# Seven products instead of eight for five pairs of slices of a feed-forward layer, with helping operations placed by due times

## The chip, the cores and the metric

The program runs on one core of one Trainium2 chip (the kernel is built for a single core). The metric is device time in microseconds (us) of one execution; several executions are given by their median.

The engines are named as in the profile: PE is TensorE (matrix products), DVE is VectorE, ACT is ScalarE, POOL is GpSimd, SP is SyncE, which issues the DMA transfers.

## The reference

Attention over clusters gives 1536 tokens of 512 numbers; two feed-forward layers follow. Both are shown whole, as the change and the stretches of time around it lie in them.

```python
def _moe_ref(x, w_in, w_out):                      # layer 1: 512 -> 2048 -> 512
    h = x @ w_in
    beta = 1.0
    neg = h <= -beta
    pos = h >= beta
    g = np.where(pos, h, np.where(neg, 0.0, (h + beta) ** 2 / (4.0 * beta)))
    return (g @ w_out).astype(np.float32)

def _moe2_ref(x, w_gate, w_val, w_out, rms_g):     # layer 2: 512 -> 1536 -> 512
    rms = np.sqrt(np.mean(x * x, axis=-1, keepdims=True) + 1e-06)
    xn = x / rms * rms_g
    g = xn @ w_gate
    silu = g * (1.0 / (1.0 + np.exp(-g)))
    val = xn @ w_val
    return (silu * val @ w_out).astype(np.float32)
```

## The kernel before, in words

**Numbers in two parts.** Every fp32 operand of a product is held as a high and a low part of type fp32r. One product of a 128-row stationary tile with 512 columns is three matmuls: high by high, high by low, low by high.

**Tiles.** The tokens lie in three blocks of 512 (`NB`, `BLK`), numbered 0, 1 and 2. Layer 1 has 16 slices of 128 hidden units, layer 2 has 12. `h_unit(layer, m, b)` makes slice m of the hidden units for block b: four 128-row pieces of X times three, 12 matmuls into one PSUM bank (`proj`, L624). Then come the gate on ACT (L639, L640) and DVE (L641), the rounding to a high part on ACT (L668) and the low part on DVE (L665). `y_unit` multiplies the results of a group of slices with slices of the second matrix, for 128 tokens at a time (L786 to L788); the sum over groups is kept in SBUF in Y (ACT copies the first group, L800, DVE adds the later ones, L802). The groups of layer 1 are `GROUPS1`.

**Weights.** SP loads every slice of a weight matrix twice, 512 KB each, once as it is (`raw`, L521) and once shifted by two bytes (`mid`, L523). There are two buffers for each, and a slice's conversion must end before the next load into its buffers can start. The conversion takes one ACT and six DVE operations (L565, then L566, L568, L570, L576, L578, L580) and puts the slice into one of 24 SBUF places.

**Layer 2 already multiplies in seven products.** Blocks 0 and 1 against the two halves of the contraction and two weight slices would take eight half products; sums and differences of X and of the weights make seven do (`term_unit`, with the table `TERMS`; PE line L651). The sums of the weights are made on POOL by `w_sums` (L534, 256 columns wide), and the parts on ACT and DVE (L557, L559). Partial results that are used twice are copied from PSUM to SBUF by ACT (L713, names u, e, v, w) and added in by DVE (L716) and by POOL (L719). Layer 1 uses none of this: POOL stands still through most of it.

**Order.** All engines run their own queues in the order in which the program writes the instructions. A list of units (`units`) sets the order on PE; the helping operations are written between them by a pace: so much of DVE's time (`pace["dve"]`, `cost`, `fill`) for so much of PE's, with stages of a unit's follow-up work in `later`, released by `drain`.

## Time and profile before

| | us |
|---|---|
| median of 3 executions (lowest, highest) | 777.17 (776.75, 777.27) |
| the profiled execution | 775.95 |
| its span in the trace | 774.2 |
| busy: PE, DVE, ACT, POOL | 768.3, 609.9, 391.9, 288.9 |
| layer 1 begins on PE at | 230.5 |

The granted TensorE clock is 0.999 over the span. A line of the timeline reads: start in us after the start of the span, duration in us, engine, line of the program, operation, output<-inputs, shape, and in brackets how long the engine had been idle and what ended that. `aa`, `bb` and `place` are SBUF places of converted slices or of gated results; `raw`, `mid` and `bits` belong to a conversion in progress; `h`, `y`, `A`, `B`, `E` are PSUM banks.

### The profile page before, as it was taken

How to read it: one execution, taken by the hardware profiler on the slowest of the kernel's cores; microseconds unless marked ns; L12 is line 12 of the kernel's file. 1: busy time of each engine (PE TensorE's matmuls, PEld its weight loads, DVE VectorE, ACT ScalarE, POOL GpSimd, SP SyncE). 2: the span in 40 equal slices, each digit the busy share in tenths (PEclk: the TensorE clock that was granted, in tenths of full speed). 3: DMA queues.
4: the chain of work that ended last, by engine and by line, in shares of the span. 5: the costliest groups of instructions: out<-in, count | busy, mean ns of one | idle time of the engine just before them, and what ended most of it. 6: DMA issues, size and time to landing. Idle time of an engine off the chain costs nothing.

```text
span 774.2 us, 10868 instructions
## 1 busy us (share of the span) xinstructions
PE 768.3 (99%) x3714; PEld 592.0 (76%) x3714; DVE 609.9 (79%) x1106; ACT 391.9 (51%) x758; POOL 288.9 (37%) x313
## 2 busy tenths in 40 slices
PE   8999999999999999999999999999999999999998
PEld 4666666776558888888888888878888888888887
DVE  6776887776578999877668768899999799988743
ACT  7676767665567655444334447544545315423430
POOL 5878999998000000000001206441454334423400
PEclk9999999999999999999999999999999999999999
DMA  7657665573144676444334310125563343434013
GB/s 202 173 138 182 156 150 131 150 172 113 55 142 143 218 237 218 170 137 163 109 109 136 99 37 0 32 95 181 187 213 109 104 160 128 154 109 163 1 41 123
DMA packets 32679, 103.41 MB, mean 134 GB/s; under 512 B 5016, under 2 KB 5356, under 8 KB 32624
## 3 DMA queue, kind: packets, MB, share of 16 engines
q1 hardware_dynamic: 32612, 102.72, 43.8%
q8 instruction: 29, 0.48, 0.3%
q14 instruction: 26, 0.21, 0.1%
q10 hardware_dynamic: 12, 0.00, 0.0%
HBM read 81.02 MB, written 3.15 MB: 109 GB/s over the span
## 4 chain that ended last, share of the span: by engine, by line
PE 92%; DVE 2%; ACT 2%; DMA 1%; POOL 1%; issue 1%; ACTq 0%; DVEq 0%; POOLq 0%
PE h L624 25%; PE y L788 9%; PE y L787 9%; PE y L786 9%; PE pv L406 8%; PE B L651 8%; PE mp L336 5%; PE sc L385 4%; PE sc L386 4%; PE E L651 4%; PE A L651 2%; PE sum L425 1%; DMA kraw<-kT 1%; PE simt L171 1%; PE sum L414 1%
## 5 line engine op out<-in xcount | busy, mean ns | idle before, releaser
L338 DVE TENSOR_REDUCE M<-mp 128x1 f32<-128x384 f32 x186 | 94.6, 552 | 44.6 <-PE mp L336 44.4
L534 POOL TENSOR_TENSOR bits<-place 128x256 f32<-128x256 f32 x18 | 17.6, 1000 | 265.5 <-DVE place L580 265.5
L398 POOL TENSOR_TENSOR acc<-acc,P 128x384 f32<-128x384 f32 x112 | 109.2, 1004 | 4.1 <-ACT P L388 3.5
L388 ACT ACTIVATE P<-sc 128x384 f32<-128x384 f32 x192 | 82.3, 490 | 42.1 <-PE sc L386 34.1
L624 PE MATMUL h<-xh,aa 128*128 128x512 f32 x280 | 89.3, 390 | 0.1
L802 DVE TENSOR_TENSOR Y<-y,Y 128x512 f32<-128x512 f32 (+1 forms) x85 | 57.8, 681 | 39.6 <-PE y L788 39.3
L639 ACT ACTIVATE a<-h,half_b 128x512 f32<-128x512 f32 x48 | 33.0, 687 | 81.4 <-PE h L624 80.4
L406 PE MATMUL pv<-P,v 128*64 128x384 f32 x384 | 70.6, 492 | 0.0
L385 PE MATMUL sc<-aa,bb 112*128 112x384 f32 x192 | 66.1, 344 | 0.0
L386 PE MATMUL sc<-aa,bb 97*128 97x384 f32 x192 | 65.0, 338 | 0.0
L624 PE MATMUL h<-xh,bb 128*128 128x512 f32 x200 | 64.2, 389 | 0.0
L624 PEld LDWEIGHTS h<-xh,aa 128*128 128x128 f32 x280 | 52.5, 188 | 12.9 <-DVE a L641 0.8
L565 ACT ACTIVATE raw<-raw 128x512 f32<-128x512 f32 x62 | 42.2, 680 | 38.1 <-DMA raw<-w_out 12.4
L641 DVE SCALAR_TENSOR_TENSOR a<-h,a 128x512 f32<-128x512 f32 x48 | 33.1, 690 | 29.7 <-ACT a L640 29.7
L624 PE MATMUL h<-xl,aa 128*128 128x512 f32 x140 | 54.5, 389 | 0.0
L568 DVE SCALAR_TENSOR_TENSOR bits<-raw,bits 128x512 uint32<-128x512 uint32 x68 | 51.7, 760 | 1.6
L336 PE MATMUL mp<-bb,aa 112*128 112x384 f32 x186 | 52.5, 360 | 0.3
L406 PEld LDWEIGHTS pv<-P,v 128*64 128x64 f32 x384 | 25.4, 136 | 31.4 <-issue 30.3
L336 PEld LDWEIGHTS mp<-bb,aa 112*128 112x128 f32 x186 | 32.2, 189 | 15.3 <-issue 5.5
L624 PEld LDWEIGHTS h<-xh,bb 128*128 128x128 f32 x200 | 37.5, 188 | 7.8
L719 POOL TENSOR_TENSOR w<-w,e 128x512 f32<-128x512 f32 x12 | 16.8, 1396 | 60.9 <-ACT w L713 60.9
L624 PE MATMUL h<-xl,bb 128*128 128x512 f32 x100 | 38.9, 389 | 0.0
(307 smaller groups left out, 1987.3 us busy)
## 6 DMA issues: line engine op xcount, KB each, us to landing
...
```

The source lines that it names most:

```text
L336: nc.tensor.matmul(mp, A[0:112, h, 0, 128 * qt:128 * qt + 128], Bk[0:112, h, 0, HALF * n:HALF * n + HALF], start=True, stop=True)
L338: nc.vector.tensor_reduce(st["M2", p][:, j, n:n + 1], mp, axis=AX.X, op=ALU.max)
L385: nc.tensor.matmul(sc, Bk[0:112, h, 0, ks], A[0:112, h, 0, qs], start=True, stop=False)
L386: nc.tensor.matmul(sc, Bk[0:97, h, 1, ks], A[0:97, h, 1, qs], start=False, stop=True)
L388: nc.scalar.activation(P, sc, AF.Exp, scale=0.125)
L398: nc.gpsimd.tensor_tensor(acc, acc, P, op=ALU.add)
L406: nc.tensor.matmul(pv[64 * h:64 * h + 64, 0:HALF], st["v", p][:, h, kt], st["P", p, i, h], start=(kt == 0), stop=(kt == NT - 1))
L624: nc.tensor.matmul(h, w[:, wi, fs], x[:, kc, cs], start=(n == 0), stop=(n == 11))
L651: nc.tensor.matmul(h, w[:, wi, fs], x[xi][:, kc], start=start and n == 0, stop=(n == 5), skip_group_check=not start)
L786: nc.tensor.matmul(y[:, c], g[:, 0, fs], w[:, 0, c], start=(m == m0), stop=False)
L787: nc.tensor.matmul(y[:, c], g[:, 0, fs], w[:, 1, c], start=False, stop=False)
L788: nc.tensor.matmul(y[:, c], g[:, 1, fs], w[:, 0, c], start=False, stop=(m == ms[-1]))
```

## The change

Layer 1 gets the seven products for blocks 0 and 1, in five pairs of slices: (3, 4), (5, 6), (7, 8), (9, 10) and (11, 12). Block 2 and the other slices keep whole products. Per pair, two sums of POOL (512 columns, L725) and four (256 columns, L739 to L742) make the weights' sums `s1_m_0` and `s1_m_1`; ACT and DVE split each into parts (L702, L703). X needs three more sums and a changed block 1: `x_parts` makes them once (L979 and L982 on POOL, L982 and L990 on DVE, L989 on ACT), overwriting the first half of block 1's X; `x_back` restores it before the last slices of block 1 (L954 to L962). ACT copies the partial results of a pair from PSUM (L917), DVE (L923) and POOL (L928) add them in.

The conversion of a slice is done in another way: two ACT operations (L708, L709) and five DVE operations (L710 to L714).

The helping operations are no longer paced. Each is a task with a due time; while the program is built, a plan with a clock for each engine and a price for each kind of operation (`KINDS`) chooses what is written next into which queue. The units on PE are sorted by a table of numbers, `ORDER`.

```diff
-GROUPS1 = [3, 3, 4, 3, 3]
+GROUPS1 = [3, 4, 3, 3, 3]
...
-LOCK = 0.3
+AFTER = 12
+SQP = ()
+LOCKED = 1.15
+KEEP, YD, GD, ROUND, XD = 1.5, 6.0, 6.0, 6.0, 2.0
+ORDER = (
+    0, 1, 2, 3, 4, 5, 6, 7, 8, 9, 10, 11, 12, 13, 14, 15, 16, 17, 18, 19, 20, 21, 22, 23, 24, 25, 26, 27, 28,
+    29, 30, 31, 33, 34, 32, 35, 36, 37, 38, 39, 40, 41, 42, 43, 44, 45, 46, 47, 48, 49, 50, 53, 51, 52, 54,
...
+NEAR, DUE, CONV = 0.1, 8.0, 4.0
+LOAD, LAND = 4.2, 0.8
...
+             "tt": ("dve", 0.6, 0.74), "t256": ("dve", 0.335, 0.47), "tiny": ("dve", 0.08, 0.2),
+             "p512": ("pool", 1.28, 1.4), "p256": ("pool", 0.74, 0.85)}
...
+        clock[e] = at + busy * (LOCKED if e == "dve" and clock["pool"] > at else 1.0)
...
+        hi, mid, t, sq = cv.pop(n)
+        tf, bits = t.bitcast(F32), sq.bitcast(U32)
+        v = nc.vector
+        task(landed[n], op("copy", lambda: nc.scalar.activation(sq, hi.bitcast(F32), AF.Copy, scale=2.0 ** -112), (("y", n),)),
+             op("copy", lambda: nc.scalar.activation(hi.bitcast(F32), hi.bitcast(F32), AF.Sign), (("sg", n),)), due=due_of(key))
+        task(landed[n], op("t256", lambda: v.tensor_scalar(mid, mid, 0x01FFFFFF, None, op0=ALU.bitwise_and)),
+             op("t256", lambda: v.tensor_scalar(t, bits, 3, 0x7FFFF000, op0=ALU.logical_shift_left, op1=ALU.bitwise_and), (), (("y", n),)),
+             op("tt", lambda: v.tensor_tensor(w[:, 0], tf, hi.bitcast(F32), op=ALU.mult), (("w0", key),), (("sg", n),)),
+             op("t256", lambda: v.tensor_scalar(t, w[:, 0].bitcast(U32), 0xFF800000, None, op0=ALU.bitwise_and)),
+             op("tt", lambda: v.scalar_tensor_tensor(w[:, 1], mid, 2.0 ** -36, tf, op0=ALU.mult, op1=ALU.mult), (("w1", key),)),
+             due=due_of(key), end=load_next)
+        if layer == 2 and i < 2:
+            w_sums(2, i, m, key, w, tf)
+        if layer == 1 and i == 0 and GROUPS1[0] <= m < M1 - GROUPS1[-1]:
+            w_sums(1, 1 - m % 2, m - 1 + m % 2, key, w, tf)
+
...
+        first = op("p512", lambda: g(f, w[:, 0].bitcast(F32), w[:, 1].bitcast(F32), op=ALU.add), (("f", layer, i, m),), (("w0", key), ("w1", key)))
...
+        task(0.0, first, op("p256", lambda: g(tile_of(k1)[:, left], f2[:, left], f2[:, right], op=ALU.add), (), (("f", layer, 0, m),)),
+             op("p256", lambda: g(fp[k1][:, right], fp[k1][:, left], f1[:, left], op=ALU.subtract), (k1,)),
+             op("p256", lambda: g(tile_of(k2)[:, left], f1[:, left], f2[:, left], op=ALU.subtract)),
+             op("p256", lambda: g(fp[k2][:, right], f1[:, right], fp[k1][:, right], op=ALU.subtract), (k2,)), due=due_of(key))
...
+    def term_unit(layer, k, m):
         c, _, half, start = TERMS[k]
+        w = need(key_of(layer, k, m))
+        row, b = ENDS.get(k, (0, 0))
+        n = m + row if layer == 1 else m
+        if k in ENDS and (layer == 1 or row):
+            G[layer, n, b] = take()
...
+        if k in (6, 7, 4, 3):
+            wait_for(("keep", {6: "u", 7: "v", 4: "w", 3: "e"}[k], layer, m))
...
+        if k in (1, 5, 6):
+            task(now(1.36), kept("uev"[(1, 5, 6).index(k)]), due=now(1.36) + KEEP)
+            return
+        both = op("p512", lambda: nc.gpsimd.tensor_tensor(C["w", m], C["w", m], C["e", m], op=ALU.add), (("used", "e", layer, m),), (("keep", "e", layer, m),))
+        first = {2: (plus("u"),) if k == 2 else (), 3: (plus("v"),) if k == 3 else (), 7: (kept("w"), both) if k == 7 else (), 4: ()}[k]
+        end_ = ("used", "w", layer, m) if k == 7 else bank
+        if layer == 1:
+            last = gated(n, b, (lambda: C["w", m]) if k == 7 else (lambda: src), end_)
...
+    def x_parts():
...
+        def add(i, j, kc, b):
+            cs = slice(BLK * b, BLK * b + BLK)
+            nc.gpsimd.tensor_tensor(get(i, j), XH[:, kc + j, cs].bitcast(F32), XL[:, kc + j, cs].bitcast(F32), op=ALU.add)
+
+        def minus(e, i, j, x, y):
+            e.tensor_tensor(get(i, j), get(x, j), get(y, j), op=ALU.subtract)
+
+        for j in range(2):
+            dst = [(XH[:, j, b1], XL[:, j, b1]), (h3[:, j], l3[:, j]), (h2[:, j], l2[:, j]), (h4[:, j], l4[:, j])]
+
+            def hilo(i, part, j=j, dst=dst):
+                h, l = dst[i]
+                return (op("copy", lambda: nc.scalar.copy(h, get(i, j)), (("xh", i, j),), (("p", i, j),)),
+                        op("tt", lambda: nc.vector.tensor_tensor(l, get(i, j), h.bitcast(F32), op=ALU.subtract), (("xt", part, j),)))
+
+            g, v = nc.gpsimd, nc.vector
+            task(now(0.0), op("p512", lambda j=j: add(1, j, 0, 1)), op("p512", lambda j=j: add(0, j, 0, 0)),
+                 op("p512", lambda j=j: minus(g, 0, j, 1, 0), (("p", 0, j),)), due=now(0.0) + XD + 0.1 * j)
+            task(now(0.0), *hilo(0, 1), due=now(0.0) + XD + 0.1 * j)
+            task(now(0.0), op("p512", lambda j=j: add(2, j, 2, 1), (), (("p", 0, j),)),
+                 op("tt", lambda j=j: minus(v, 1, j, 2, 1), (("p", 1, j),)),
+                 op("tt", lambda j=j: minus(v, 2, j, 2, 0), (("p", 2, j),)), due=now(0.0) + XD + 0.1 * j)
+            task(now(0.0), *hilo(1, 3), due=now(0.0) + XD + 0.2)
+            task(now(0.0), *hilo(2, 2), due=now(0.0) + XD + 0.2)
+            task(now(0.0), op("p512", lambda j=j: add(3, j, 2, 0), (), (("p", 0, j),)),
+                 op("p512", lambda j=j: minus(g, 3, j, 3, 2), (("p", 3, j),), (("p", 2, j),)), *hilo(3, 4), due=now(0.0) + XD + 0.2)
...
+        def pair_of(m):
+            g, s, r = (1, 0, m), (1, 0, -m - 1), (1, 1, -m - 1)
+            return [term(1, 1, m), h(1, m, 2), term(1, 2, m), end(g), term(1, 5, m), term(1, 6, m), end(s), h(1, m + 1, 2), term(1, 3, m), term(1, 7, m), end(r)]
+
+        def last_pair(m):
+            return [term(1, 4, m), end((1, 0, m + 1))]
...
+        hz = [h(1, m, b) for b in range(NB) for m in range(GROUPS1[0])]
+        yield from (*hz[:7], xs(0), *hz[7:], *(done(1, m) for m in range(GROUPS1[0])))
+        zs = ys(1, 0)
+        yield from zs
+        a, b, c, d, e = (pair_of(m) for m in range(3, 13, 2))
+        yield from (*a, b[0], *last_pair(3), *b[1:])
+        zs = ys(1, 1)
+        yield (tables, 0.0, 0.0, [], 0)
+        yield from (zs[0], *last_pair(5), *zs[1:], *c, d[0], *last_pair(7), *d[1:])
+        zs = ys(1, 2)
+        yield from (zs[0], *last_pair(9), *zs[1:], *e)
         n = len(GROUPS1) - 1
         new = range(sum(GROUPS1[:n]), M1)
-        yield from (*ys(1, n - 1, 0), *hs(1, new, 0), *ys(1, n - 1, 1), *hs(1, new, 1), *ys(1, n, 0))
+        hz, ws = hs(1, new, 0), ys(1, n - 1, 0)
+        yield from (hz[0], *last_pair(11), back(0), back(1), hz[1], hz[2], *ws, *ys(1, n - 1, 1), *hs(1, new, 1), *ys(1, n, 0))
...
+    work[:] = [work[i] for i in ORDER]
```

Three places show what that does to the queues. The first is POOL after the last product of attention (`acc6_7_1`, L421; L398 before). Before:

```order
L398 TENSOR_TENSOR acc6_7_1_2571<-acc6_7_1_2571,P6_11_1_2658 128x384
L534 TENSOR_TENSOR bits32_4430<-place3_3131 128x256 x2
L534 TENSOR_TENSOR bits33_4459<-bb0_106 128x256 x2
L534 TENSOR_TENSOR s0_0_4565<-bits33_4459 128x256
L534 TENSOR_TENSOR s0_0_4565<-s0_0_4565,bits32_4430 128x256
L534 TENSOR_TENSOR s0_1_4566<-bits32_4430,bits33_4459 128x256
L534 TENSOR_TENSOR s0_1_4566<-bits32_4430,s0_0_4565 128x256
```

and with the change:

```order
L979 TENSOR_TENSOR p1_0_3160<-xh_103,xl_104 128x512
L979 TENSOR_TENSOR p1_1_3162<-xh_103,xl_104 128x512
L979 TENSOR_TENSOR p0_0_3164<-xh_103,xl_104 128x512
L979 TENSOR_TENSOR p0_1_3182<-xh_103,xl_104 128x512
L982 TENSOR_TENSOR p0_0_3164<-p1_0_3160,p0_0_3164 128x512
L982 TENSOR_TENSOR p0_1_3182<-p1_1_3162,p0_1_3182 128x512
L979 TENSOR_TENSOR p2_0_3218<-xh_103,xl_104 128x512
L979 TENSOR_TENSOR p2_1_3224<-xh_103,xl_104 128x512
L979 TENSOR_TENSOR p3_0_3241<-xh_103,xl_104 128x512
L979 TENSOR_TENSOR p3_1_3246<-xh_103,xl_104 128x512
L982 TENSOR_TENSOR p3_0_3241<-p3_0_3241,p2_0_3218 128x512
L982 TENSOR_TENSOR p3_1_3246<-p3_1_3246,p2_1_3224 128x512
```

Before, the next work after attention was a sum for layer 2. Now the twelve additions for X come first (p0 to p3, two halves each); behind them stand the sums `bits6` and `bits7` of slices 3 and 4 (L725, 512 columns) and the first pair's four short ones (L739 to L742).

The second is DVE where slice 3 of w_in (`raw6`, the first of the first pair) is converted. Before:

```order
L566 TENSOR_SCALAR bits6_3139<-raw6_3137 128x512
L568 SCALAR_TENSOR_TENSOR bits6_3139<-raw6_3137,bits6_3139 128x512
L570 TENSOR_SCALAR mid6_3138<-mid6_3138 128x512
L641 SCALAR_TENSOR_TENSOR a1_1_2_3164<-h1_1_2_3151,a1_1_2_3164 128x512
L576 SCALAR_TENSOR_TENSOR aa1_107<-raw6_3137,bits6_3139 128x512
L578 TENSOR_SCALAR bits6_3139<-aa1_107 128x512
L641 SCALAR_TENSOR_TENSOR a1_2_2_3183<-h1_2_2_3170,a1_2_2_3183 128x512
L665 TENSOR_TENSOR aa1_107<-a1_1_2_3164,aa1_107 128x512
L580 SCALAR_TENSOR_TENSOR aa1_107<-mid6_3138,bits6_3139 128x512
```

and with the change:

```order
L982 TENSOR_TENSOR p1_0_3160<-p2_0_3218,p1_0_3160 128x512
L982 TENSOR_TENSOR p2_0_3218<-p2_0_3218,p0_0_3164 128x512
L982 TENSOR_TENSOR p1_1_3162<-p2_1_3224,p1_1_3162 128x512
L990 TENSOR_TENSOR place0_3128<-p1_0_3160,bb1_108 128x512
L982 TENSOR_TENSOR p2_1_3224<-p2_1_3224,p0_1_3182 128x512
L990 TENSOR_TENSOR bb1_108<-p2_0_3218,bb1_108 128x512
L990 TENSOR_TENSOR place0_3128<-p1_1_3162,bb1_108 128x512
L990 TENSOR_TENSOR bb1_108<-p2_1_3224,bb1_108 128x512
L990 TENSOR_TENSOR place2_3130<-p3_0_3241,place1_3129 128x512
L849 TENSOR_TENSOR place4_3132<-a1_2_2_3197,place4_3132 128x512
L990 TENSOR_TENSOR place2_3130<-p3_1_3246,place1_3129 128x512
L712 TENSOR_TENSOR aa1_107<-bits6_3139,raw6_3137 128x512
```

L825 is a gate, L849 a low part of a gated result. The four differences (L982) and the low parts (L990) of X are new and stand ahead of the conversion's product (L712); of the instructions from `bits5` (L569) to the last difference on DVE, p2_1 (L982), fifteen do not read PSUM and four are gates that do.

The third is ACT behind the copies Y of the first group's first tiles. Before:

```order
L800 COPY Y_3125<-y1_0_2_0_3234 128x512
L800 COPY Y_3125<-y1_0_3_0_3249 128x512
L565 ACTIVATE raw9_3228<-raw9_3228 128x512
L639 ACTIVATE a1_3_0_3284<-h1_3_0_3271,half_b_93 128x512
L640 ACTIVATE a1_3_0_3284<-a1_3_0_3284 128x512
L565 ACTIVATE raw10_3262<-raw10_3262 128x512
L639 ACTIVATE a1_3_1_3309<-h1_3_1_3296,half_b_93 128x512
L640 ACTIVATE a1_3_1_3309<-a1_3_1_3309 128x512
```

and with the change, where `s1_3_0` and `s1_3_1` are the first pair's sums:

```order
L702 CAST aa2_109<-s1_3_0_3349 128x512
L702 CAST aa2_109<-s1_3_1_3362 128x512
L1090 COPY Y_3125<-y1_0_9_0_3352 128x512
L708 ACTIVATE raw8_3312<-raw8_3312 128x512
L709 ACTIVATE raw8_3312<-raw8_3312 128x512
L1090 COPY Y_3125<-y1_0_10_0_3370 128x512
L708 ACTIVATE raw11_3332<-raw11_3332 128x512
L1090 COPY Y_3125<-y1_0_11_0_3386 128x512
L709 ACTIVATE raw11_3332<-raw11_3332 128x512
L917 COPY u1_3_3414<-B1_3_3407 128x512
```

and, following on that without a gap (`u1_3`, `e1_3`, `v1_3` are the first pair's kept partial results, `raw12` is a slice of w_out, `s1_5_0` the second pair's first sum):

```order
L814 ACTIVATE a1_3_2_3448<-h1_3_2_3418,half_b_93 128x512
L821 ACTIVATE a1_3_2_3448<-a1_3_2_3448 128x512
L708 ACTIVATE raw12_3399<-raw12_3399 128x512
L851 CAST bb0_106<-a1_3_2_3448 128x512
L917 COPY e1_3_3460<-E1_3_3453 128x512
L814 ACTIVATE a1_3_0_3478<-A1_3_3441,half_b_93 128x512
L702 CAST bb2_110<-s1_5_0_3450 128x512
L917 COPY v1_3_3474<-B1_3_3407 128x512
```

The casts of the first pair's sums now stand ahead of copies and conversions that before followed directly, and the copy `v1_3` stands behind the cast of the second pair's first sum. On PE, the 12 tiles of Y (9 matmuls each) are followed by the pair's products in this order: B1_3 (6 matmuls), h1_3_2 (12), A1_3 (6), E1_3 with `s1_3_0` (6), B1_3 with `s1_3_0` (6, after `u1_3`), E1_3 with `s1_3_1` (6, after `e1_3`), B1_3 with `s1_3_1` (6, after `v1_3`).

In numbers, the program for PE has 3,395 matmul instructions instead of 3,425, DVE 1,080 instructions instead of 1,108, ACT 851 instead of 749, POOL 347 instead of 318, and SP the same 329.

## Rows read from the trace of the kernel before

**Rows 1.** The page, parts 1 and 4: engines, and the chain of waits by line
```profile
PE 768.3 (99%) x3714; PEld 592.0 (76%) x3714; DVE 609.9 (79%) x1106; ACT 391.9 (51%) x758; POOL 288.9 (37%) x313
...
PE 92%; DVE 2%; ACT 2%; DMA 1%; POOL 1%; issue 1%; ACTq 0%; DVEq 0%; POOLq 0%
```

**Rows 2.** Windows: us, then busy us of PE, PEld, DVE, ACT, POOL, clock, DMA
```profile
500.00:520.00 20.00, 19.81 (x89) 15.23 (x89) 18.86 (x28) 10.48 (x20) 10.05 (x10) 1.00 0.23 79
540.00:560.00 20.00, 20.00 (x90) 16.57 (x89) 19.62 (x30) 9.67 (x17) 9.96 (x10) 1.00 0.59 199
230.00:418.00 188.00, 188.00 (x831) 155.29 (x828) 152.25 (x279) 96.50 (x158) 0.00 (x0) 1.00 0.49 162
```

**Rows 3.** Timeline of PE: start, duration (us); blocks' first matmuls
```profile
249.66 0.39 PE L786 MATMUL y<-bb 128*128 128x512 f32 x1
...
257.82 0.39 PE L624 MATMUL h<-xh,aa 128*128 128x512 f32 x1
...
265.98 0.39 PE L786 MATMUL y<-bb,bb 128*128 128x512 f32 x1
```

**Rows 4.** VectorE's costliest groups by line, 230 to 418 us: busy us, mean ns
```profile
L641 DVE SCALAR_TENSOR_TENSOR a<-h,a 128x512 f32<-128x512 f32 x37 | 25.5, 690 | 19.7 <-ACT a L640 19.7
L568 DVE SCALAR_TENSOR_TENSOR bits<-raw,bits 128x512 uint32<-128x512 uint32 x29 | 20.0, 689 | 0.6
L802 DVE TENSOR_TENSOR Y<-y,Y 128x512 f32<-128x512 f32 x25 | 17.1, 687 | 11.6 <-PE y L788 11.5
```

**Rows 5.** Timeline of POOL with VectorE idle or on PSUM operands
```profile
472.12 1.29 POOL L665 TENSOR_TENSOR bb<-a,bb 128x512 fp32r<-128x512 f32 x1 [1.38 <-ACT bb L668]
...
474.92 0.74 POOL L764 TENSOR_TENSOR xl<-t,xh 128x256 fp32r<-128x256 f32 x1
475.62 0.74 POOL L764 TENSOR_TENSOR aa<-t,bb 128x256 fp32r<-128x256 f32 x1
```

**Rows 6.** Timeline of POOL: 512-wide additions beside VectorE
```profile
537.41 1.68 POOL L719 TENSOR_TENSOR w<-w,e 128x512 f32<-128x512 f32 x1 [16.42 <-ACT w L713]
...
592.10 1.43 POOL L719 TENSOR_TENSOR w<-w,e 128x512 f32<-128x512 f32 x1 [6.87 <-ACT w L713]
```

**Rows 7.** Timeline of DVE: the instructions beside the additions of group 6
```profile
537.99 1.40 DVE L578 TENSOR_SCALAR bits<-bb 128x512 uint32<-128x512 uint32 x1
...
592.41 1.67 DVE L580 SCALAR_TENSOR_TENSOR place<-mid,bits 128x512 fp32r<-128x512 uint32 x1
```

**Rows 8.** The page, part 5: POOL's 256-wide sums beside VectorE, mean ns
```profile
L534 POOL TENSOR_TENSOR bits<-place 128x256 f32<-128x256 f32 x18 | 17.6, 1000 | 265.5 <-DVE place L580 265.5
```

**Rows 9.** Timeline of DVE beside six 256-wide POOL sums, 561 to 568 us
```profile
561.54 1.12 DVE L568 SCALAR_TENSOR_TENSOR bits<-raw,bits 128x512 uint32<-128x512 uint32 x1
...
567.65 0.69 DVE L568 SCALAR_TENSOR_TENSOR bits<-raw,bits 128x512 uint32<-128x512 uint32 x1
```

**Rows 10.** Timeline of DVE at the end of attention and the start of layer 1
```profile
243.49 0.43 DVE L578 TENSOR_SCALAR bits<-aa 128x512 uint32<-128x512 uint32 x1
243.96 0.69 DVE L580 SCALAR_TENSOR_TENSOR aa<-mid,bits 128x512 fp32r<-128x512 uint32 x1
244.56 0.69 DVE L665 TENSOR_TENSOR bb<-a,bb 128x512 fp32r<-128x512 f32 x1
...
249.79 0.42 DVE L570 TENSOR_SCALAR mid<-mid 128x512 uint32<-128x512 uint32 x1
250.12 0.68 DVE L641 SCALAR_TENSOR_TENSOR a<-h,a 128x512 f32<-128x512 f32 x1
```

**Rows 11.** Timeline of ACT in layer 1's first blocks
```profile
247.99 0.68 ACT L565 ACTIVATE raw<-raw 128x512 f32<-128x512 f32 x1
248.55 0.68 ACT L639 ACTIVATE a<-h,half_b 128x512 f32<-128x512 f32 x1
...
254.81 0.70 ACT L565 ACTIVATE raw<-raw 128x512 f32<-128x512 f32 x1 [0.28 <-DMA raw<-w_in]
```

**Rows 12.** Timeline of SyncE: a load of raw
```profile
251.48 0.33 SPq L521 DMA_DIRECT2D raw<-w_in  x1
```

524 lines of the change are left out of this document (332 added, 192 removed), and 16 rows, old and new, of the table ORDER.

## Prediction

> **What bounds the kernel now.** I read the page first: PE is busy 768.3 of 774.2 us, and the chain of waits runs through PE for 92% of the span [rows 1]. Then the windows: from 230 to 418 us, most of layer 1, PE is busy all 188 us at the full clock, VectorE 152.25, ScalarE 96.50, GpSimd not at all; in layer 2's windows, where seven products are in use already, GpSimd works half of the time and VectorE 18.9 to 19.6 of 20 us, and PE still loses at most 0.19 us in 20 [rows 2]. So a matmul fewer is time gained, as long as the other engines deliver in time, and layer 1 offers an idle GpSimd for it.
>
> What a matmul costs is the pitch on PE, not the 0.39 us of a row: from 249.66 to 257.82 lie four tiles of Y, 36 matmuls, and from there to 265.98 three products of 12, again 36; 8.16 / 36 = 0.2267 us [rows 3].
>
> **The gain.** Four products of 12 matmuls become seven of 6: 48 - 42 = 6 fewer per pair, 30 in five pairs, which is also what the two programs differ by. 30 x 0.2267 = 6.80 us. Nothing else is taken from PE. VectorE loses one 512-wide operation per conversion: L568, 20.0 us for 29 in this stretch [rows 4]. It lies beside PE and gives nothing back directly. ScalarE's added operation per conversion, its copies and casts lie beside PE too, in 188 - 96.50 = 91.5 us of idle time [rows 2]; only their order counts, below. SP issues the same loads.
>
> **The prices of the helpers.** A 512-wide GpSimd addition takes 1.29 us where VectorE does not disturb it, a 256-wide one 0.70 from start to start [rows 5]. Beside VectorE both suffer: GpSimd's addition took 1.68 and 1.43 us [rows 6], and of the VectorE operations in those moments one took 1.40 us, against 0.43 of the same line alone [rows 7, 10], and one 1.67 against 0.69 [rows 7, 10]. Both times about 0.98 us was added. So I charge 0.98 us for a 512-wide addition to whatever VectorE does next, bounded below by what the windows show on average and above by the addition's whole 1.29. The average: in 540 to 560 us VectorE's 30 operations took 19.62, in the quiet stretch 279 took 152.25, or 0.546 each [rows 2]; 19.62 - 30 x 0.546 = 3.2 for 9.96 us of GpSimd, and by the same working 3.6 for 10.05 in 500 to 520. About 0.35 us per us of GpSimd is 0.45 per wide addition. I take 0.98, because x_parts packs its additions as closely as in those moments, not as loosely as in a window. Short sums in company average 1.00 us [rows 8], and six of them stretched VectorE operations of some 2.9 us alone to 6.1 us [rows 9], 0.53 each.
>
> The Trainium skill, page "SBUF — State Buffer", section "Who interferes with whom", says that VectorE and GpSimd share a port pair by an exclusive lock held for a whole instruction, and that a VectorE instruction with two SBUF inputs fully blocks against a GpSimd one that reads SBUF. The trace agrees in kind, with 0.98 of 1.29 us. By that rule each wide addition would add its 1.29 us, and the result would come out near 778.4.
>
> Alone, a two-input VectorE operation follows the next in 0.60 us (243.96 to 244.56), a one-input one in 0.33 (249.79 to 250.12) [rows 10]. A ScalarE operation takes 0.56 from start to start (247.99 to 248.55) [rows 11].
>
> **The chain in front of the first pair.** The additions for X can start once slice 5's high part is done, 243.5 [rows 10]. Up to the last of the twelve, VectorE has to get through fifteen instructions that do not read PSUM (twelve at 0.60, three at 0.33 to 0.43), because the last difference on GpSimd needs VectorE's: 8.3 us. With twelve additions at 0.98 = 11.8 the X parts are complete at 243.5 + 8.3 + 11.8 = 263.6; the plan, which lengthens VectorE by a factor of 1.15 only, has the additions done at 243.5 + 12 x 1.28 = 258.9. Five more low parts end at 266.6. Slice 3's five remaining operations take 2.2: 268.8; PE wants it at 249.66 + 108 x 0.2267 = 274.1, in time. Slice 4's last three and one addition's charge, 1.5 + 1.0: 271.3. Its own sum 1.29: 272.6. Two short sums at 1.0: s1_3_0 at 274.6, two more: s1_3_1 at 276.6, and its cast on ScalarE ends at 277.2.
>
> Now ScalarE's queue, in order. Eight operations at 0.56 follow up to u1_3: 281.7. PE wants it 30 matmuls after 274.1, at 280.9: 0.8 late. The third of the eight, the sign of raw8, ends at 278.9; VectorE then ends that conversion in 1.5, at 280.4, and only then are the buffers free for the load of raw12. Issue to first use was 251.48 to 254.81, 3.3 us, with ScalarE waiting for it [rows 11, 12]: raw12 is there at 283.7. The ScalarE queue stands until then; its copy, a cast and e1_3 end at 285.4. PE wants e1_3 at 274.1 + 36 x 0.2267 = 282.3: 3.1 late. Slice 6's sign, the seventh of the eight, ends at 281.1; three VectorE operations and one charge: 283.6; its sum 1.29 and two short ones: s1_5_0 at 286.9. Its cast and behind it v1_3 end at 288.0. PE wants v1_3 42 matmuls after 274.1, at 283.7: **4.3 us late** in all; the earlier lags are inside it. What is late next: products of block 2 and then tiles of Y stand behind on PE, ready long before, so PE runs on.
>
> After the first pair I charge nothing: later sums of weights have several slices of time, VectorE has 0.69 us less per conversion, and layer 2's windows show PE fed at heavier loads [rows 2]. That cover is what the last rival takes away. x_back's six additions lie before the slices 13 to 15 of block 1, with about 96 matmuls (21.8 us of PE) between them and the first product that reads the result, against 6 x 1.29 = 7.7; conversions of layer 2 change by the same removed operation. Two unknown costs remain: the sign operation and the scaled copy on ScalarE, taken as any 512-wide ScalarE operation.
>
> **Sum.** Profiled execution 775.95 - 6.80 + 4.3 = 773.45. The median stands 1.22 above it (777.17), so 774.7. The twelve charges are the largest term in the chain; 0.13 us either way in each (under half of the way from 0.98 to 1.29) moves it by 1.6: own range 773.1 to 776.3.
>
> **Rivals.** What a measurement can tell from no change is about 0.2%, 1.55 us: faster is below 775.6, slower above 778.7.
>
> *The first pair is in time (0.23).* If the additions hold VectorE only 0.45 us each, as the windows' average has it, GpSimd itself sets the end: 243.5 + 12 x 1.29 = 259.0, 4.6 us earlier, and v1_3 comes at 283.4, before its 283.7. Then all 6.80 us are kept: 770.4, or 770.2 with the 0.19 us that PE lacks at 500 to 520. For it: operations that read PSUM, such as L641 and L802, keep their 690 and 687 ns [rows 4] and can run beside an addition. Against it: fifteen of nineteen of the instructions here do not read PSUM.
>
> *The waits are longer (0.14).* An addition that holds VectorE for its whole 1.29 us adds 12 x 0.31 = 3.7 us to the chain, wait 8.0: 777.17 - 6.80 + 8.0 = 778.4, no change. For it: 1.29 is the addition's own time [rows 5]; against it: neither moment shows more than 0.98 added [rows 7].
>
> *Slower: VectorE runs out of time over all of layer 1 (0.18).* In 230 to 418 it is busy 152.25; it loses 20.0 (L568) and gains 32 operations of 0.68 (12 for X, and for each of five pairs two low parts and two additions), 21.8: 154.1. GpSimd brings 12 + 10 + 5 wide additions at 0.98 and 20 short ones at 0.53: 37.1. Together 191.2 in 188 - 6.8 = 181.2 us. If every charge falls on an operation that needs SBUF, PE waits 10.0 us: 777.17 - 6.80 + 10.0 = 780.4. It decides from the share of the charges that lands: at 0.73 VectorE is full, at 0.95 the kernel is slower than before by over 0.2%. For it: the plan counts 15%, the rows show more than a doubling. Against it: 72 of the operations (L641, L802 and the ten new additions, some 49 of the 154 us) read PSUM, which leaves a share of 0.68, 179.3 us; and the windows' 0.35 per us of GpSimd gives 17.
>
> That the change does not save the matmuls is no rival here: their count in the program says it does.
>
> **Numbers.** The forecast has 0.45, the rivals 0.23, 0.14 and 0.18. Of the forecast's own range two thirds lie below 775.6 (0.30), the rest is within 0.2%. Faster 0.30 + 0.23 = 0.53; same 0.15 + 0.12 = 0.27; slower 0.18 + 0.02 = 0.20. The range runs from 770.2 to 778.9, leaving out the last rival's 0.18. It holds cases of both signs; the likeliest one's own range is the 773.1 to 776.3 above.
>
> **What would show it.** Right: in the profile after, PE idles once, between 280 and 290 us, some 4 us, with ScalarE's copy L917 as releaser, and GpSimd's additions from 243.5 on take until about 264, with L982 and L990 on VectorE at 1.5 us and more. The first rival shows them ended by 260 and PE without a gap; the last shows VectorE above 97% in all windows of layer 1 and PE gaps at conversions (L712, L714) throughout. I am wrong altogether if the gaps lie in layer 2 or at the change of layers, where I charge nothing.

## The result, and the profile after

| | before | with the change |
|---|---|---|
| median, us (lowest to highest) | 776.96 (776.19 to 777.27) | 783.58 (783.38 to 784.70) |
| executions | 4 | 4 |
| ratio of the runs | | 1.0091 (95%: 1.0075 to 1.0107) |
| profiled span, us | 774.2 | 781.6 |

The change makes the kernel slower by 0.9%, some 7 us (7.1 by the ratio, 6.6 by the medians). The forecast of 774.7 was wrong, in sign too. First the page of the kernel after, parts 1 and 4.

```profile
PE 767.1 (98%) x3684; PEld 589.2 (75%) x3684; DVE 614.7 (79%) x1078; ACT 448.2 (57%) x860; POOL 345.2 (44%) x342
...
PE 81%; DVE 10%; ACT 4%; POOL 2%; issue 2%; DMA 1%; DVEq 0%; ACTq 0%; POOLq 0%
```

PE is busy 767.1 us instead of 768.3 [rows 1], although 30 matmuls, 6.8 us, are gone: part of what is left runs slower. In the chain of waits VectorE's share has risen from 2% to 10%. The view of what PE waited for (us in total, times, longest) names the places; before, no row of this view was above 0.4 us, except 1.0 us at the very start.

```profile
PE E L834 <- ACT e L917: 5.2, 2, 3.3
PE B L834 <- ACT u L917: 1.5, 1, 1.5
PE y L1078 <- DVE place L849: 1.1, 1, 1.1
```

The timeline of PE shows the first pair, with the row that ends each wait (start, duration, and in brackets the wait and its releaser), and the windows of 2 us the clock in the same stretch (columns as in rows 2).

```profile
269.87 0.50 PE L1078 MATMUL y<-aa,place 128*128 128x512 f32 x1 [1.10 <-DVE place L849]
...
284.87 1.66 PE L834 MATMUL B<-bb,aa 128*128 128x512 f32 x6 [1.53 <-ACT u L917]
289.83 0.79 PE L834 MATMUL E<-xh,aa 128*128 128x512 f32 x1 [3.31 <-ACT e L917]
...
295.40 0.57 PE L775 MATMUL h<-xh,aa 128*128 128x512 f32 x1
```

```profile
290.00:292.00 2.00, 2.00 (x5) 1.61 (x6) 1.77 (x3) 0.85 (x2) 1.92 (x3) 0.50 0.77 291
...
296.00:298.00 2.00, 2.00 (x10) 1.64 (x10) 2.00 (x3) 1.97 (x4) 1.35 (x1) 1.00 0.21 57
```

PE stands 1.10 us for a low part that a tile of Y needs, 1.53 us for u and 3.31 us for e. Behind that the granted clock is 0.50, TensorE's lower level of 1.2 GHz, until after 295.4: the 12 matmuls from 289.83 to 295.40 take 5.57 us instead of 12 x 0.2267 = 2.72, so 2.85 us more are lost. Two waits of 0.4 us follow at tiles of Y near 427, and at the change of layers 1.88 us for the copy of e of layer 2's first slice, again with a granted clock of 0.50 behind it (18 matmuls from 502.64 to 508.48 take 5.84 us instead of 4.08). The row that ends this wait, and a window behind it:

```profile
502.64 0.50 PE L834 MATMUL E<-xh,aa 128*128 128x512 f32 x1 [1.88 <-ACT e L917]
```

```profile
505.00:506.00 1.00, 1.00 (x4) 0.71 (x4) 0.93 (x5) 0.00 (x0) 0.00 (x0) 0.50 0.04 16
```

Waits 8.62, clock 2.85 + 1.76: 13.2 us lost, 6.8 saved, 6.4 more; of the 7.4 us between the spans the first tile of Y has 0.68 already, as it begins at 250.34 instead of 249.66. This sum is book-keeping of the one profiled execution; how much of the half clock is a price of its own is taken up below.

Why u and e are late is read from the other engines. GpSimd's timeline, X's sums and the first sum of the weights:

```profile
244.03 1.50 POOL L979 TENSOR_TENSOR p<-xh,xl 128x512 f32<-128x512 f32 x1 [48.15 <-ACT bb L851]
...
262.94 1.61 POOL L982 TENSOR_TENSOR p<-p,p 128x512 f32<-128x512 f32 x1 [3.22 <-DVE p L982]
265.85 1.61 POOL L982 TENSOR_TENSOR p<-p,p 128x512 f32<-128x512 f32 x1 [1.29 <-DVE p L982]
```

VectorE's in the same stretch:

```profile
244.39 1.68 DVE L571 SCALAR_TENSOR_TENSOR aa<-mid,bits 128x512 fp32r<-128x512 uint32 x1
...
246.60 0.68 DVE L825 SCALAR_TENSOR_TENSOR a<-h,a 128x512 f32<-128x512 f32 x1
247.97 1.72 DVE L849 TENSOR_TENSOR bb<-a,bb 128x512 fp32r<-128x512 f32 x1 [0.69 <-ACT bb L851]
...
255.56 1.54 DVE L710 TENSOR_SCALAR mid<-mid 128x512 uint32<-128x512 uint32 x1
...
265.03 0.68 DVE L982 TENSOR_TENSOR p<-p,p 128x512 f32<-128x512 f32 x1
...
287.96 0.68 DVE L825 SCALAR_TENSOR_TENSOR a<-h,a 128x512 f32<-128x512 f32 x1
```

ScalarE's:

```profile
278.48 0.62 ACT L702 CAST aa<-s 128x512 fp32r<-128x512 f32 x1 [7.49 <-POOL s L740]
...
284.24 0.57 ACT L917 COPY u<-B 128x512 f32<-128x512 f32 x1
...
288.68 0.62 ACT L851 CAST bb<-a 128x512 fp32r<-128x512 f32 x1 [1.55 <-DVE a L825]
289.20 0.58 ACT L917 COPY e<-E 128x512 f32<-128x512 f32 x1
```

X's twelve sums run from 244.03 to 267.46. Beside them eight of VectorE's operations, up to its last difference at 265.03, take 1.5 to 1.8 us instead of 0.42 to 0.69, and GpSimd stands 3.22 and 1.29 us for VectorE's differences. ScalarE stands 7.49 us for the first sum of the weights, with later slices' conversions behind it in its queue, and then 1.55 us at the cast of block 2's gated slice, which waits for VectorE's gate of 287.96. The copy of e stands behind that cast.

### The profile page after: what moved, and what is told of

Same layout as the page of the kernel before. It is cut to its first block, busy times and chain, and to the rows that moved or that the text cites. A ratio compares the mean times of both kernels' runs of the same rounds, so it can differ in the third digit from the quotient of the medians.

```text
span 781.6 us, 10939 instructions
## 1 busy us (share of the span) xinstructions
PE 767.1 (98%) x3684; PEld 589.2 (75%) x3684; DVE 614.7 (79%) x1078; ACT 448.2 (57%) x860; POOL 345.2 (44%) x342
## 4 chain that ended last, share of the span: by engine, by line
PE 81%; DVE 10%; ACT 4%; POOL 2%; issue 2%; DMA 1%; DVEq 0%; ACTq 0%; POOLq 0%
PE h L775 13%; PE B L834 10%; PE pv L429 8%; PE y L1078 8%; PE y L1076 8%; PE y L1077 8%; PE E L834 5%; PE mp L359 5%; PE sc L408 4%; PE sc L409 4%; PE A L834 2%; DVE a L825 2%; PE sum L448 1%; ACT a L814 1%; PE simt L194 1%
## 5 line engine op out<-in xcount | busy, mean ns | idle before, releaser
L421 POOL TENSOR_TENSOR acc<-acc,P 128x384 f32<-128x384 f32 x112 | 109.5, 1011 | 4.2 <-ACT P L411 3.5
L775 PE MATMUL h<-xh,aa 128*128 128x512 f32 x232 | 75.7, 391 | 0.1
L928 POOL TENSOR_TENSOR w<-w,e 128x512 f32<-128x512 f32 x17 | 24.2, 1422 | 113.7 <-ACT w L917 113.7
L725 POOL TENSOR_TENSOR bits<-aa 128x512 f32<-128x512 f32 x17 | 23.5, 1380 | 94.8 <-DVE aa L714 94.8
L775 PEld LDWEIGHTS h<-xh,aa 128*128 128x128 f32 x232 | 43.7, 188 | 11.2 <-DVE a L825 0.8
L708 ACT ACTIVATE raw<-raw 128x512 f32<-128x512 f32 x62 | 41.8, 678 | 17.1 <-DMA raw<-w_in 6.0
L775 PE MATMUL h<-xl,aa 128*128 128x512 f32 x116 | 45.2, 389 | 0.0
L709 ACT ACTIVATE raw<-raw 128x512 f32<-128x512 f32 x62 | 41.9, 680 | 1.0
L711 DVE TENSOR_SCALAR bits<-raw 128x512 uint32<-128x512 uint32 x62 | 39.2, 633 | 1.2 <-ACT raw L708 1.1
L775 PE MATMUL h<-xh,bb 128*128 128x512 f32 x120 | 39.4, 389 | 0.0
L408 PEld LDWEIGHTS sc<-aa,bb 112*128 112x128 f32 x192 | 36.3, 189 | 3.1 <-ACT P L411 1.4
L710 DVE TENSOR_SCALAR mid<-mid 128x512 uint32<-128x512 uint32 x62 | 37.6, 609 | 1.0 <-DMA mid<-w_val 0.8
L725 POOL TENSOR_TENSOR bits<-place 128x512 f32<-128x512 f32 x8 | 11.3, 1414 | 59.5 <-DVE place L714 59.5
```

Source lines behind the costliest of these rows:

```text
L408: nc.tensor.matmul(sc, Bk[0:112, h, 0, ks], A[0:112, h, 0, qs], start=True, stop=False)
L421: nc.gpsimd.tensor_tensor(acc, acc, P, op=ALU.add)
L775: nc.tensor.matmul(h, w[:, wi, fs], x[:, kc, cs], start=(n == 0), stop=(n == 11))
```

## The experiments

**The new plan and conversion without the pairs (e4_plan_without_pairs).**

```diff
-        a, b, c, d, e = (pair_of(m) for m in range(3, 13, 2))
-        yield from (*a, b[0], *last_pair(3), *b[1:])
+        for n in range(1, len(GROUPS1) - 1):
...
+            for m in range(m0, m0 + g):
+                ks += [[h(1, m, b)] for b in range(NB)]
```

> The new plan and the new conversion alone: layer 1 has whole products everywhere, as in the kernel before, so PE has the 30 matmuls (6.8 us) back, and X's sums, the weights' sums and the copies of layer 1 are gone. If the loss comes from the pairs' helping work: no waits in layer 1, what is left is the wait at the change of layers (1.9 us and about 2 us at half clock): 778 to 780. If the plan or the conversion itself feeds PE worse: waits all over layer 1, 785 or more.

779.71 us, ratio 1.0045 (1.0028 to 1.0062). PE's waits (us in total, times, longest):

```profile
PE E L832 <- ACT e L915: 1.9, 1, 1.9
PE xt L1134 <- DVE Y L1127: 1.1, 1, 1.1
```

There is no wait in layer 1. So the conversion with two ScalarE operations and the planned order feed layer 1 as well as before; at the change of layers they lose 3.0 us with nothing gained for it.

**X's sums on VectorE (e1_x_on_vector).**

```diff
-            nc.gpsimd.tensor_tensor(get(i, j), XH[:, kc + j, cs].bitcast(F32), XL[:, kc + j, cs].bitcast(F32), op=ALU.add)
+            nc.vector.tensor_tensor(get(i, j), XH[:, kc + j, cs].bitcast(F32), XL[:, kc + j, cs].bitcast(F32), op=ALU.add)
```

> The twelve sums and differences for X are made on VectorE instead of GpSimd (and the plan, which prices them there, orders the queues anew). If the two engines holding each other up in these sums starts the loss: VectorE needs 12 x 0.60 = 7.2 us for them where the pair of engines lost about 12, the first pair's sums come about 4 us earlier, PE's waits of 1.1, 1.5 and 3.3 us near 268, 284 and 288 us shrink to under 1 together, TensorE keeps its full clock there, and the time falls from 783.6 by about 8 to 775 to 776. The rival, that VectorE simply has no time left in layer 1: 12 more operations on it make the waits longer, 784 or more.

779.61 us, ratio 1.0047 (1.0032 to 1.0062): about 3.4 us better than the change (1.0091), where some 8 were expected. X's sums end at 263.23 instead of 267.46 although VectorE makes all of them (1.27 us of that are there at the first tile of Y already), and L571 and the L849 behind it take 0.69 us. The waits of 1.1 and 1.5 us are gone and the clock in the first pair is full, but e still comes 2.79 us late, and two new waits at tiles of Y take 1.5 us, the longer 1.11 us at 310. The plan also chose another order here, so the 3.4 us are not the engine's alone. ScalarE's timeline, and VectorE's, show why:

```profile
284.80 0.62 ACT L851 CAST bb<-a 128x512 fp32r<-128x512 f32 x1 [2.94 <-DVE a L825]
285.33 0.58 ACT L917 COPY e<-E 128x512 f32<-128x512 f32 x1
```

```profile
280.55 1.54 DVE L711 TENSOR_SCALAR bits<-raw 128x512 uint32<-128x512 uint32 x1
...
284.08 0.68 DVE L825 SCALAR_TENSOR_TENSOR a<-h,a 128x512 f32<-128x512 f32 x1
```

The cast stands 2.94 us for the gate of 284.08, and that stands behind the conversion of a slice, one operation of which GpSimd's sum of weights stretches to 1.54 us.

**Matmuls into the wait (e3_filler).**

```diff
-        product(C[c, m], w, 256 * half, x_of(*x) if x else fp["xt"][{6: 0, 7: 1, 4: 2}[k]], start)
+        for _ in range(3 if layer == 1 and m == 3 and k == 5 else 1):
+            product(C[c, m], w, 256 * half, x_of(*x) if x else fp["xt"][{6: 0, 7: 1, 4: 2}[k]], start)
```

> The product E of the first pair with its first sum is run three times instead of once (the result is the same): 12 more matmuls, 2.7 us, where PE waits 1.5 and 3.3 us anyway. If the half clock after the long wait is a cost of its own: the wait for e is about 2 us instead of 3.3, the clock stays full, and the kernel is 2 to 3 us faster in spite of 12 more matmuls, 780.5 to 781.5. If the clock costs nothing: 783.6 to 784.5, the work merely fills the wait.

782.15 us, ratio 1.0078 (1.0063 to 1.0093). The windows of the same stretch:

```profile
290.00:292.00 2.00, 2.00 (x6) 1.24 (x4) 1.60 (x3) 0.94 (x2) 1.92 (x4) 0.50 0.59 240
...
294.00:296.00 2.00, 2.00 (x10) 1.67 (x9) 1.80 (x4) 2.00 (x5) 0.09 (x1) 1.00 0.00 0
```

The wait for u is gone, the one for e is 2.42 us, and the clock falls all the same, for a shorter time (12 matmuls from 289.36 to 293.98, 4.62 us, lose 1.9 instead of 2.85). With 12 more matmuls the kernel is not slower than the change; the intervals overlap, so how much of that is the clock is not settled.

**True prices in the plan (e2_true_prices).**

```diff
-LOCKED = 1.15
+LOCKED = 2.4
-             "p512": ("pool", 1.28, 1.4), "p256": ("pool", 0.74, 0.85)}
+             "p512": ("pool", 1.5, 1.62), "p256": ("pool", 0.85, 0.96)}
```

> Only numbers of the plan change: GpSimd's additions are priced at 1.5 and 0.85 us, and VectorE beside GpSimd 2.4 times as long instead of 1.15. The X sums stay on GpSimd and end as late as before, but ScalarE's queue has the copies u and e of the first pair ahead of conversions that wait. If the order of ScalarE's queue turns lateness into PE's waits: the waits of 1.5 and 3.3 us fall to 1 or less together, the full clock stays, 776 to 778. If the lateness of the X sums alone decides: the same waits, 783 to 784.

788.30 us, ratio 1.0156 (1.0138 to 1.0174), slower still. PE's largest waits:

```profile
PE y L1076 <- ACT aa L851: 4.5, 2, 3.2
PE xt L1136 <- DVE Y L1129: 2.2, 1, 2.2
...
PE E L834 <- ACT e L917: 1.0, 2, 0.5
```

At the first pair 0.52 us is left for e, as hoped. But at 311 to 316 us PE stands 2.7 us for a slice of w_out that is converted later now and 3.2 us for the high part of a gated result, whose gate VectorE does behind another conversion; 2.2 us follow at the change of layers. The order moved the wait, not the lateness.

**A slice of block 2 between (e7_slice_between).**

```diff
-    29, 30, 31, 33, 34, 32, 35,
+    29, 30, 31, 32, 33, 34, 35,
```

> Only the table of the order on PE: block 2's product of slice 4 (12 matmuls, 2.7 us) goes ahead of the first pair's product with the second sum. If e is late whatever PE does: the wait of 3.3 us shrinks by 2.7, the clock stays full (another 2.9 us), and the time falls by 5 to 6: 777.5 to 778.5. If the wait only moves to the next copy, v, or w: 782 or more.

782.61 us, ratio 1.0078 (1.0058 to 1.0098). The wait for e falls from 3.3 to 0.62, and v (1.22) and w (2.85) are waited for instead.

**The copies first**, alone (e5_copies_first) and with X's sums on VectorE (e6_vector_and_copies). The diff shows what both have; the first also puts the copy of e ahead of the cast of the second pair's first sum.

```diff
-        return (op("copy", lambda: nc.scalar.copy(g[:, 0], fp["g", m, b]), stage=1),
+        after_e = (("keep", "e", 1, m),) if layer == 1 and b == NB - 1 and m in (3, 5, 7, 9, 11) else ()
+        return (op("copy", lambda: nc.scalar.copy(g[:, 0], fp["g", m, b]), (), after_e, stage=1),
...
+            after_e = (("keep", "e", 2, 0),) if m == 0 and k == 2 else ()
+            last = (op("copy", lambda: silu(m, b, src), (bank, ("a", m, b)), after_e),)
```

> The changed kernel with ScalarE's order altered at two places: a pair's copy of e goes ahead of the cast of block 2's gated slice and of the second pair's first sum, and in layer 2's first slice ahead of the silu of A. The X sums stay on GpSimd. If the queue in front of e makes PE wait: the wait of 1.9 us at the change of layers goes, with the half clock behind it (together 3 to 4 us), and the first pair's 3.3 us fall to about 1.8, as the copy of a slice of w_out with its load stays ahead; 5 us less, 778 to 779.5. If e is late because PE or the weights' sums are: the same waits, 783 to 784.

> Both remedies: X's sums on VectorE as in e1_x_on_vector, and the copies of e first. In e1_x_on_vector the cast of the gated slice waited 2.9 us for VectorE with e behind it. If these two places are the whole loss beside the saved matmuls: the waits of 2.8 and 1.8 us and the half clock go, 5 to 6 us under e1_x_on_vector, 773 to 774.5, which is faster than the kernel before by 0.2 to 0.4%. If the saved time comes back elsewhere (VectorE full): waits at tiles of Y grow, 777 or more.

786.73 us (1.0135, 1.0116 to 1.0155) and 788.94 us (1.0159, 1.0138 to 1.0180): both worse than without. PE's largest waits of the second:

```profile
PE y L1078 <- DVE aa L712: 3.5, 2, 1.9
PE xt L1138 <- DVE Y L1131: 3.3, 1, 3.3
PE B L834 <- ACT v L918: 2.7, 1, 2.7
```

In the second the wait for e is gone, and in its place PE stands for v, for the w_out slices near 311 to 316 us, and for the normalised Y at the change of layers.

**The change of layers.** The copy of e put ahead of the silu, in the kernel without pairs (the second part of the diff above, alone; e8_plan_and_copies):

> e4_plan_without_pairs with e ahead of the silu in layer 2's first slice. If the change of layers is all that the new plan loses there: its wait of 1.9 us goes, and the time falls from 779.7 to 777 to 778, within 1.5 us of the kernel before. If the new conversion or the plan costs something else: 779 or more.

779.09 us, ratio 1.0040 (1.0025 to 1.0055), no gain:

```profile
PE xt L1135 <- DVE Y L1128: 3.3, 1, 3.3
```

The 1.9 us for e and the 1.1 us for the norm's output became 3.3 us for the norm's output. What is late is the norm on VectorE. In the kernel before, the last sum of squares is there at 492.42 + 0.19 and the norm's operations begin 1.7 us later:

```profile
494.27 0.70 DVE L836 TENSOR_SCALAR ssq<-ssq 128x4 f32<-128x4 f32 x1
```

With the change the last sum of squares ends at 497.91 + 0.19, and the norm begins 3.9 us later, behind a conversion that GpSimd's 512-wide sum holds up (1.69 us for L712, 0.85 for L713):

```profile
498.30 1.69 DVE L712 TENSOR_TENSOR bb<-bits,raw 128x512 fp32r<-128x512 f32 x1
500.03 0.85 DVE L713 TENSOR_SCALAR bits<-bb 128x512 uint32<-128x512 uint32 x1
...
501.99 0.16 DVE L1117 TENSOR_SCALAR ssq<-ssq 128x4 f32<-128x4 f32 x1
```

The copy of e is late by the same conversion: ScalarE's silu, which stands ahead of it, waits for the addition of u on VectorE (L923 at 500.79).

```profile
501.51 0.60 ACT L856 ACTIVATE a<-A 128x512 f32<-128x512 f32 x1 [2.95 <-DVE A L923]
```

Putting that conversion behind the norm, in the changed kernel (e11_norm_first) and with X's sums on VectorE (e15_vector_and_norm),

```diff
-                (("w0", key),), (("sg", n),)),
+                (("w0", key),), (("sg", n), ("rr", 2)) if n == 48 else (("sg", n),)),
```

> At the change of layers the conversion of the slice that VectorE does between the sums of squares and the norm of block 2 (its last three operations, and with them GpSimd's sum) is put behind the norm. e5_copies_first and e8_plan_and_copies showed the wait of 1.9 us for e move to a wait of 3.3 us for the normalised Y, so the norm is what is late there: the norm begins 3 us earlier, both waits shrink to under 1 us, and the half clock goes: 783.6 - 1.9 - 2.0 = 779.7. If the change of layers is bound by something behind (the slice is then late itself): 782 or more.

> X's sums on VectorE (e1_x_on_vector) and the slice at the change of layers behind the norm (e11_norm_first). If the two losses are separate, they add: 779.6 - 1.8 - 1.5 = 776.3, level with the kernel before. If what is put off at the change of layers comes back later, as e11_norm_first showed at 546 us: 778 or more.

gave 783.33 us (1.0090, 1.0073 to 1.0107) and 779.86 us (1.0046, 1.0031 to 1.0061). The wait at the change of layers is 0.93 us and the clock there stays full, but a tile of Y stands 1.2 us at 543 to 546 for a low part, and in the first of the two v is 0.57 us late in the first pair. By the time nothing is gained: 1.0090 against 1.0091 of the change, 1.0046 against 1.0047 with the sums on VectorE.

**Shorter sums; four pairs.** `w_sums`' first operation in two halves of 256 columns; and slices 3 and 4 as whole products, without the order table in layer 1 (e10_halves and e12_four_pairs; of each, the main line of the edit):

```diff
-        first = op("p512", lambda: g(f, w[:, 0].bitcast(F32), w[:, 1].bitcast(F32), op=ALU.add), (("f", layer, i, m),), (("w0", key), ("w1", key)))
+        first = (op("p256", half(left), (), (("w0", key), ("w1", key))), op("p256", half(right), (("f", layer, i, m),)))
```

```diff
-        a, b, c, d, e = (pair_of(m) for m in range(3, 13, 2))
+        b, c, d, e = (pair_of(m) for m in range(5, 13, 2))
```

> The first sum of each weight slice on GpSimd (128x512) is made in two halves of 256 columns, as before; nothing else. If GpSimd holds VectorE for a whole instruction, shorter ones hold shorter: VectorE's 1.5 to 1.7 us operations beside L725 become 1.0 to 1.2, but there are twice as many of them; total time the same within 1.5 us, 782 to 785. If only the long ones do harm at the change of layers (VectorE's 1.69 and 1.28 us there): 2 us less.

> Slices 3 and 4 get whole products again, four pairs are left (24 matmuls or 5.44 us saved instead of 6.80), X's sums begin 18 us later and the order on PE in layer 1 is the plain one without the table. If X's sums are a one-off price that has to fit into what VectorE has to spare before its first readers, more time or less load helps: waits before 330 us of 0 to 3 us instead of 5.9, 778 to 781. If the budget of the whole layer is short: waits of 5 us and more in any case, 783 or more.

785.55 us (1.0123, 1.0107 to 1.0138) and 792.07 us (1.0204, 1.0188 to 1.0219). In the first, VectorE's L712 at the change of layers takes 1.12 us instead of 1.69, as expected, but e is 3.38 us late in the first pair and a tile of Y near 427 stands 2.49 us: narrower sums alone do not help. In the second u is 5.24 us late and a tile 2.99 us; as it also lost the table, it does not tell the budget from the order.

**X's sums left out, planned anew (e9_no_x_sums).** The parts are made from block 0's X without the 16 sums and differences.

> Leaves part of the computation out: x_parts makes no sums or differences (12 on GpSimd, 4 on VectorE); the casts and the low parts are made of block 0's X instead, so the parts have other values. All the rest is as in the changed kernel. If the sums, some 12 x 1 + 4 x 0.6 = 14 us of VectorE's time and as much of GpSimd's, are what layer 1 begins too late with: no wait over 0.5 us from 260 to 330, the full clock, and 783.6 - 1.1 - 1.5 - 3.3 - 2.9 = 774.8. If the pairs' other helping work (sums of the weights, copies, additions) is too much as well: waits of 3 us or more stay at the first two pairs, 778 or more.

780.77 us, ratio 1.0059 (1.0044 to 1.0074). By the number this is the second outcome, but the second pair has no wait: the wait at 269 and VectorE's long operations are gone, but u is 0.98 and e 4.03 us late. ScalarE's timeline:

```profile
280.18 0.62 ACT L702 CAST bb<-s 128x512 fp32r<-128x512 f32 x1 [3.68 <-POOL s L740]
...
287.75 0.62 ACT L851 CAST bb<-a 128x512 fp32r<-128x512 f32 x1 [2.05 <-DVE a L825]
288.27 0.58 ACT L917 COPY e<-E 128x512 f32<-128x512 f32 x1
```

The plan, which knew of less work, put the second pair's sums ahead of u and more conversions ahead of the gate. This run could not tell a late X from a bad order, so the next two keep the order.

**The same left out, every queue in the changed kernel's order.** The plan still counts the operations, but they are not issued (e13_sums_unissued):

```diff
-            e.tensor_tensor(get(i, j), get(x, j), get(y, j), op=ALU.subtract)
+            get(i, j)
...
-                return (op("copy", lambda: nc.scalar.copy(h, get(i, j)), (("xh", i, j),), (("p", i, j),)),
+                x = XH[:, (0, 0, 2, 2)[i] + j, 0:BLK].bitcast(F32)
+                return (op("copy", lambda: nc.scalar.copy(h, x), (("xh", i, j),), (("p", i, j),)),
```

The second (e14_all_sums_unissued) leaves out layer 1's sums of the weights too:

```diff
-        g = nc.gpsimd.tensor_tensor
+        g = nc.gpsimd.tensor_tensor if layer == 2 else (lambda *a, **k: None)
```

> Leaves part of the computation out: X's 12 GpSimd sums and 4 VectorE differences are not issued, and the parts are made of block 0's X. Unlike in e9_no_x_sums the plan still counts them, so every other instruction stands in its queue exactly where it stands in the changed kernel. If VectorE and GpSimd being late against the plan (X's sums were complete at 267.5 instead of 259) is what makes PE wait: no wait over 0.5 us from 260 to 330 and no half clock there, 783.6 - 8.8 = 774.8. If the order of the queues makes e late even when X is in time, as in e9_no_x_sums: waits of 3 to 5 us for u and e stay, 780 to 782.

> As e13_sums_unissued, and GpSimd's sums of layer 1's weights (10 of 512 and 20 of 256 columns) are not issued either; their casts read X's block 0. Leaves those parts of the computation out. All queues keep their order. Of GpSimd's work in layer 1 only the five additions of partial results are left. If the holding up by GpSimd is the whole cause: no waits before 430 us, 774 to 775, and the change of layers keeps its 1.9 us. If ScalarE's added operations are the cause as well: waits for ACT of 2 us and more stay in the first two pairs.

775.03 us, ratio 0.9987 (0.9976 to 0.9997), and 772.80 us, ratio 0.9960 (0.9945 to 0.9974). PE's waits of the first, and of the second:

```profile
PE E L834 <- ACT e L917: 1.8, 1, 1.8
PE B L834 <- ACT v L917: 1.2, 1, 1.2
PE xt L1137 <- DVE Y L1130: 1.1, 1, 1.1
```

```profile
PE E L834 <- ACT e L917: 1.9, 1, 1.9
PE xt L1137 <- DVE Y L1130: 1.1, 1, 1.1
```

In the first, ScalarE's copies come where PE needs them, in the same order as in the change:

```profile
277.36 0.58 ACT L917 COPY u<-B 128x512 f32<-128x512 f32 x1
...
282.33 0.58 ACT L917 COPY e<-E 128x512 f32<-128x512 f32 x1
...
285.20 0.58 ACT L917 COPY v<-B 128x512 f32<-128x512 f32 x1
```

u 6.9, e 6.9 and v 6.9 us earlier than in the change; the waits for u and e in the first pair are gone, one of 1.2 us for v is left, and the clock is full throughout. Without the sums of the weights that one goes too. What stays in both is the change of layers.

**The account.** In us against the kernel before, from the ratios times 776.5: the plan without pairs +3.5. With the pairs' 6.8 us saved that would be -3.3, and the change without any of these sums measures -3.1. The sums of the weights cost 2.1 (to -1.0), and X's sums 8.1, to the +7.1 of the change. Each ratio carries about 1 us either way, so the 8.1 stands and the 2.1 is little more than its own error. The 8.1 holds everything that X's sums bring with them: their length, the held operations, the waits behind them and the half clock.

## Why the prediction was wrong

**The gain** was right: 30 matmuls, 6.8 us. The run without the sums and the run without pairs differ by 6.6.

**The price of an addition** was right in size, but not in number. L571 took 1.68 instead of 0.69 and L710 1.54 instead of 0.42 beside the additions: 0.99 and 1.12 us, where 0.98 was charged. Up to VectorE's last difference eight operations were held in this way, not twelve; that difference itself (265.03) took 0.68 us, as GpSimd stood waiting for it. The Trainium skill, page "SBUF — State Buffer", section "Who interferes with whom", adds that a VectorE instruction with one SBUF input outside the two-port modes does not contend; L825, which reads PSUM and one SBUF tile, kept its 0.68 us in the same stretch (246.60). L710 has one SBUF input as well and was held, so this alone did not decide here. The rows 4 that the prediction names for this could not show it: GpSimd does nothing in that stretch [rows 2].

**The chain in front of the first pair** is the step that failed first, and with the half clock behind it, it turned the sign. "The X parts are complete at 263.6": 267.46 measured. The step added up fifteen operations of VectorE (8.3 us) and twelve charges (11.8 us). The charges were too many, 8.5 us measured. But three things had no term: the four gates L825 between those operations (2.4 us); the idle time of VectorE before L849 at 247.97 (0.69) and twice more (0.69 and 0.76), since the gates go back and forth between VectorE and ScalarE; and GpSimd's last addition, which starts only behind VectorE's last difference and ends 1.75 us after it (265.71 to 267.46). One member of the queue behind was missing too: ahead of e's copy ScalarE stood 1.55 us for the gate of 287.96, which VectorE does behind a conversion, and the step had counted that cast without a wait. s1_3_0 was there at 278.45 (274.6 forecast), u's copy at 284.81 (281.7), e's at 289.78 (285.4), v's at 292.63 (288.0). By the forecast PE was to leave the pair's product B with `s1_3_1` at 288.0 + 6 x 0.2267 = 289.4; it left it at 295.40, 6.0 us later. That turns the 2.5 us that the sum had left over (6.80 - 4.3) into a loss of 3.5. Of the 6.0, 0.68 was there at the first tile of Y, 1.10 is the wait at a tile of Y that the step did not name (its low part, L849, stood behind X's low parts in VectorE's queue), 0.54 is the waits for the copies (4.84 instead of 4.3), 2.85 is half clock; 0.8 is not broken down.

**The clock** had no step at all. In the profiled execution it stands for 2.85 us behind the first pair's waits and 1.76 at the change of layers. As a price of its own it is less, by an amount that stays open. The four executions of the change had mean granted clocks of 0.993, 0.998, 0.996 and 0.993 and took 783.43, 783.38, 783.72 and 784.70 us: the one with the least half clock is as slow as the profiled one. In the first pair v's copy ended at 292.63, and PE at half clock came to it at 292.68; at full clock it would have come some 1.4 us earlier and waited.

**"After the first pair I charge nothing"** is the second step that failed, at the place that the prediction itself named as the one that would prove it wrong altogether. The change of layers cost 1.88 us and 1.76 in clock, and the run without pairs shows that the new plan and conversion lose there with the pairs or without. By the sums above the change would still be slower than before without this loss, by some 3.5 us. "Layer 2's windows show PE fed at heavier loads" read a mean for a moment: what counted was one conversion between the sums of squares and the norm, and the 3.9 us that passed there instead of 1.7.

**The rivals.** The first pair in time, 0.23: fell. The waits are longer, 0.14: its X parts would be complete at 263.6 + 3.7 = 267.3, which is what was measured, but by coincidence; no operation was held for 1.29 us, 1.12 was the most, and eight were held, not twelve. VectorE out of time over all of layer 1, 0.18: its result, 780.4, was the nearest, but not its mechanism. From 300 to 420 us PE has no wait, and VectorE is busy about 88%. It runs short only where X's sums come in, until 316 us; the runs that changed the order (e2, e5, e6, e7) all found the same few microseconds, or more, at another place, which fits a local shortage but does not prove one.

**What stays open.** Whether an order exists in which the pairs pay for X's sums: none of those tried does. How much of the 8.1 us is VectorE held by GpSimd, and how much is the sums' own length: moving them to VectorE gave back 3.4, but with another order. Whether X's sums could begin earlier was not tried; in the trace the first one stands until ScalarE's cast L851 of 243.33 has ended.
